# Gate and noise matrices laid out by the host function, the table's VectorE operations given out one at a time, four value loads in one slot

## The chip, the cores and the metric

The kernel runs on one NeuronCore of one Trainium2 chip. Its engines are called here PE (TensorE, with PEld for its weight loads), DVE (VectorE), ACT (ScalarE), POOL (GpSimd) and SP (SyncE, which only issues DMAs). The metric is the device time of one execution, in microseconds. A hardware profile of one execution gives start and duration of each instruction and what ended the wait before it.

## The reference

Two stages follow each other. First attention over 8 batches, 8 heads, 576 positions and head size 64: heads 0 to 3 see a window of the last 32 positions ("plain"), heads 4 to 7 every fourth of the last 128 ("dilated"). The result is then 4608 tokens of 512 values, which go to two of eight experts each:

```python
logits = x @ w_gate
noise_scale = np.log1p(np.exp(x @ w_noise))
noisy_logits = logits + noise_scale * noise
top2 = np.argpartition(-noisy_logits, 2, axis=1)[:, :2]
...
        h = np.maximum(x[mask] @ w1[e], 0.0)
        out[mask] += top2_w[mask, k, None] * (h @ w2[e])
```

`w_gate` and `w_noise` are 512x8, `noise` is 4608x8, `w1` 8x512x1024, `w2` 8x1024x512, all float32.

## The kernel before, in words

**Attention (0 to about 200 us).** Four units of two batches; each unit has two groups, the even one dilated (keys `kd`, values `vd`), the odd one plain (`kp`, `vp`); each group has three steps. So there are 24 steps, numbered from 0, and step 3 is the first of the first plain group. The main loop (L1015 to L1047) writes the engines' orders out by hand, several steps interleaved. In its turn a step does the following.

- `qk`: two matmuls write the mask into the score tile `s` (L361), then 48 small ones add keys times queries (L372). DVE takes the maximum `mx` (L377) and writes `a = s - mx` (L378); `a` has a single buffer.
- `expo`: ACT takes the exponential of `a` (L384). `ptr`: PE transposes it into `pp` (L398), ACT copies it to `pt` (L399).
- `pv`: values times `pt` into `o` (L416); then DVE's `den`, reciprocal and scaled `x` (L423, L425, L428). `x` has three buffers.
- two slots later `x` is copied in part by ACT (L436), stored to the DRAM scratch `xs` (L441, L443), transposed by PE (L451) and multiplied by the gate and noise matrix `wg` (L473).

Between these pieces stand calls of `micro` (nine a step) and two of `fillers`. `fillers(kb)` runs what `at(kb, f)` has put down for slot `kb` (two slots a step): loads for later groups, the setups and the starts of generators. `micro` gives the generators in the list `gens` turns, in their order in the list: after a `yield 0` a generator goes on, after `yield 1` it rests to the next slot, after `yield 3` the next generator has the turn. The generators build, for the tokens whose gate values are there, noisy logits, the two best experts and the positions in each expert's list, and POOL scatters these (L630) into the DRAM table `tab`, of 37376 rows of four words.

**SP's queue.** SP issues its DMAs in the order of the program. Each waits for the one eight places before it to land, besides its own conditions (buffers free, data ready), and those behind it wait with it. The order at the start: the loads of group 0, of group 0's values, then keys and queries of group 1, and then what the slots bring.

**The setups.** `setup_a` (slot 2) clears `wg` on POOL, loads gate and noise weights into it and the noise into `nz` by three POOL DMAs (L213 to L215), with the last dimension of 8 floats as the longest contiguous run in DRAM, and makes constants. `setup_b` (slot 4) computes, in 29 DVE operations on small integer tiles `tc` (L237 to L261), the row of `xs` that belongs to each token (`tokc`). `setup_c` (slot 5) makes the rows of padding, and `pads` (slots 6, 12 and 18) writes them in three pieces to `tab` by SP (L284), through one buffer, `free`.

**Pacing.** Before a group of scatters POOL copies one element of the newest `a` or `x` to `spacer` (L307), so that POOL doesn't run ahead of the steps. That copy is a reader of `a`, for which the next writing of `a` waits.

**Experts (about 200 us to the end).** The eight experts follow one another: tokens gathered by POOL from `xs` with lists out of `tab` (L773, L781), split in two parts of lower precision, multiplied up (L829), rectified, multiplied down (L871), scaled and scattered to the output.

Of the kernel before, what the change touches and what calls it, by code (L numbers as in the profile page):

```python
# [23 lines left out]
E = 8  # L24
# [4 lines left out]
NT = T // 128  # L29
# [14 lines left out]


@with_exitstack
def attention_moe_kernel(ctx, tc, qt, kp, kd, vpl, vdl, w_gate, w_noise, noise, w1, w2, out, CAPS=(1216, 1216, 1216, 1184, 1184, 1152, 1152, 1152), SPLITS=(0, 384, 896)):
    nc = tc.nc
    tensor, vector, scalar, gpsimd, sync = nc.tensor, nc.vector, nc.scalar, nc.gpsimd, nc.sync

# [149 lines left out]
    wg = acon.tile([128, 4, 32], F32, name="wg")  # L200
    nz = gat.tile([128, NT, E], F32, name="nz")
# [7 lines left out]
    warm(NWARM)  # L209

    def setup_a():
        gpsimd.memset(wg, 0.0)
        gpsimd.dma_start(wg[:, :, 0:E], w_gate.rearrange("(c p) e -> p c e", p=128))  # L213
        gpsimd.dma_start(wg[:, :, E:2 * E], w_noise.rearrange("(c p) e -> p c e", p=128))
        gpsimd.dma_start(nz, noise.rearrange("(t p) e -> p t e", p=128))  # L215
# [12 lines left out]

    def setup_b():


        gpsimd.memset(tokc, 0)
        gpsimd.iota(tokc[:, :, 3:4], pattern=[[128, NT], [0, 1]], base=0, channel_multiplier=1)
        t = tokc[:, :, 3]
        v, s, i0, z, a = (acon.tile([128, 2, NT], I32, name=f"tc{i}") for i in range(5))
        gpsimd.iota(v[:, 0].rearrange("p (s j) -> p s j", j=3), pattern=[[0, 12], [128, 3]], base=0, channel_multiplier=1)
        vector.tensor_scalar(a[:, 0], t, 2, None, op0=OP.bitwise_and)  # L237
        vector.tensor_scalar(v[:, 1], t, 2, None, op0=OP.logical_shift_right)
        vector.scalar_tensor_tensor(v[:, 1], a[:, 0], 72.0, v[:, 1], op0=OP.mult, op1=OP.add)
        for u in range(U):  # L240
            c = slice(NG * u, NG * u + NG)
            gpsimd.iota(s[:, 0, c].rearrange("p (s j) -> p s j", j=3), pattern=[[384, 3], [0, 3]],
                        base=384 * (6 * u + 3), channel_multiplier=0)
            vector.tensor_scalar(a[:, 0, c], t[:, c], float(TU * u + S), 144.0, op0=OP.is_ge, op1=OP.mult)
            vector.scalar_tensor_tensor(v[:, 1, c], v[:, 1, c], -288.0 * u, a[:, 0, c], op0=OP.add, op1=OP.add)
            vector.memset(s[:, 1, c], 2304 * u)
        for lim in (192.0, 384.0):
            vector.tensor_scalar(z[:, int(lim) // 384], v[:, 1], lim, None, op0=OP.is_ge)
        vector.tensor_tensor(z[:, 0], z[:, 0], z[:, 1], op=OP.add)
        vector.scalar_tensor_tensor(s[:, 1], z[:, 0], 384.0, s[:, 1], op0=OP.mult, op1=OP.add)  # L250
        vector.tensor_scalar(a[:, 0], t, 1, None, op0=OP.bitwise_and)
        vector.tensor_tensor(z[:, 0], a[:, 0], z[:, 0], op=OP.subtract)
        vector.scalar_tensor_tensor(v[:, 1], z[:, 0], 192.0, v[:, 1], op0=OP.mult, op1=OP.add)

        vector.tensor_tensor(i0, v, s, op=OP.add)
        vector.tensor_scalar(a, v, 31, None, op0=OP.bitwise_and)
        vector.tensor_tensor(i0, i0, a, op=OP.add)
        vector.tensor_scalar(a, v, 32, None, op0=OP.bitwise_and)
        vector.scalar_tensor_tensor(i0, a, -31.0 / 32, i0, op0=OP.mult, op1=OP.add)
        for c in range(2):  # L260
            vector.tensor_copy(tokc[:, :, c], i0[:, c])  # L261

    def setup_c():
# [7 lines left out]
        vector.tensor_scalar(pc[:, 1:2], pc[:, 0:1], 15, None, op0=OP.bitwise_and)  # L271
        vector.tensor_scalar(pc[:, 0:1], pc[:, 1:2], float(NR), None, op0=OP.mult)
        gpsimd.iota(pr[:, 0], pattern=[[1, NR]], base=0, channel_multiplier=0)
        vector.tensor_tensor(pr[:, 0], pr[:, 0], pc[:, 0:1].to_broadcast([128, NR]), op=OP.add)
        vector.tensor_scalar(pr[:, 1], pr[:, 0], 127, None, op0=OP.bitwise_and)
        vector.tensor_scalar(pr[:, 2], pr[:, 0], OROWS - T - 1, None, op0=OP.bitwise_and)
        tr = tab.rearrange("(p t) c -> p t c", p=128)

        def pads(a, b):
            padt = free[1][:, 0:TC * (b - a)].rearrange("p (a b) -> p a b", b=TC)  # L280
            gpsimd.memset(padt, 0)
            vector.tensor_copy(padt[:, :, 0:2], pr[:, 1, a:b].unsqueeze(2).to_broadcast([128, b - a, 2]))
            vector.tensor_scalar(padt[:, :, 3], pr[:, 2, a:b], float(T), None, op0=OP.add)
            sync.dma_start(tr[:, a:b], padt)  # L284

        for i in range(3):
            at(6 + 6 * i, lambda i=i: pads(NR * i // 3, NR * (i + 1) // 3))

    gens, early = [], [True]
    room, held, rate = [0], set(), [1]  # L290
# [51 lines left out]
    slot = [0]  # L342
# [571 lines left out]
    def at(kb, *fs):  # L914
        fill.setdefault(kb, []).extend(fs)
# [3 lines left out]
    for g in range(2 * U):  # L919
        s0 = 6 * g  # L920
        if g + 1 < 2 * U:
            for i, f in enumerate(v_loads(g + 1)):
                at(s0 + 3 + 2 * (i // 2), f)
        if g + 2 < 2 * U:
            for i, f in enumerate(qk_loads(g + 2, 2)):
                at(s0 + 7 + 2 * (i // 3), f)
# [72 lines left out]
    for kc in range(4):  # L999
        a, b = ((-3, 2), (-2, 3), (4, 6), (5, 7))[kc]  # L1000
# [242 lines left out]
```

## Time and profile before

| | us |
|---|---|
| three runs | 1074.11, 1074.55, 1068.03 |
| their median | 1074.11 |
| the profiled execution | 1067.71 |
| its span | 1066.0 |
| PE busy in the span | 1001.5 (94%) |
| DVE busy | 468.1 (44%) |
| ACT busy | 319.8 (30%) |
| POOL busy | 537.6 (50%) |

Times in rows of the profile count from the start of the span. A timeline row has start, duration, engine, line, operation, output and input tiles with shapes, the count of instructions in it, and in square brackets how long the engine stood idle before it and what released it. SPq rows are DMA issues on SP's queue. A row of stretches has start and end, the length, then busy time and count for PE, PEld, DVE, ACT and POOL, the clock granted to PE, the share of time that the DMA engines were busy and what they moved.

### The profile page before, as it was taken

To read this page: it belongs to the slowest core of one execution; us is meant where nothing else is said; L and a number is where in the kernel's file an instruction comes from. 1 tells how busy PE (TensorE), PEld (TensorE's weight loads), DVE (VectorE), ACT (ScalarE), POOL (GpSimd) and SP (SyncE) were. 2 spreads that over 40 slices of the span, in tenths; PEclk is the share of its full clock that TensorE was granted. 3 is DMA by queue.
4 is the path that set the end of the run, shared out by engine and by line. 5 is a ranking of instruction groups with operands and counts; after the bars stand their busy time and mean duration, and the time that the engine had idled before them with its cause. 6 is when DMAs were issued, how large, how long until landed. Compare 5 with 4: busy or idle time off the path is not lost. (4 is left out here: it accounts for less than half of the span.)

```text
span 1066.0 us, 18824 instructions
## 1 busy us (share of the span) xinstructions
PE 1001.5 (94%) x7275; PEld 844.3 (79%) x7276; DVE 468.1 (44%) x1088; ACT 319.8 (30%) x612; POOL 537.6 (50%) x737
## 2 busy tenths in 40 slices
PE   6897887879799999999999999999999999899996
PEld 4775665758588888979897988898888888798885
DVE  7784757633144534353425343534344433333221
ACT  7664646511022312241213121312232122222110
POOL 7004244576768467555545555466455644652112
PEclk9999998989899999999999999999999999999998
DMA  8999788652336336242724262426232623443123
GB/s 283 322 335 324 247 284 283 179 209 36 70 69 140 99 57 142 56 111 52 140 42 113 51 139 43 114 50 139 47 111 55 136 51 98 95 93 80 21 29 43
DMA packets 79214, 132.95 MB, mean 125 GB/s; under 512 B 31648, under 2 KB 41296, under 8 KB 77840
## 3 DMA queue, kind: packets, MB, share of 16 engines
q1 hardware_dynamic: 56768, 92.56, 27.9%
q0 software_dynamic: 22352, 39.15, 20.3%
q8 instruction: 58, 0.95, 0.4%
q14 instruction: 36, 0.29, 0.1%
HBM read 92.11 MB, written 39.54 MB: 124 GB/s over the span
## 5 line engine op out<-in xcount | busy, mean ns | idle before, releaser
L829 PE MATMUL up<-x,w1h 128*128 128x512 f32 (+4 forms) x1536 | 393.4, 342 | 4.8 <-DVE hl L835 2.6
L781 POOL DMA_INDIRECT g<-xs,ixi x258 | 268.9, 1042 | 84.3 <-issue 79.3
L829 PEld LDWEIGHTS up<-x,w1h 128*128 128x128 f32 x1536 | 270.4, 188 | 31.1 <-DVE hl L835 3.3
L829 PE MATMUL up<-x,w1l 128*128 128x384 f32 (+4 forms) x768 | 261.9, 341 | 0.0
L871 PE MATMUL dn<-w2h,hh 128*128 128x512 f32 x576 | 226.7, 394 | 1.6 <-issue 1.5
L871 PE MATMUL dn<-w2l,hh 128*128 128x512 f32 x576 | 226.6, 393 | 1.7 <-issue 0.9
L871 PE MATMUL dn<-w2h,hl 128*128 128x512 f32 x576 | 225.9, 392 | 1.7 <-issue 1.7
L835 DVE SCALAR_TENSOR_TENSOR hl<-up,hh 128x384 fp32r<-128x384 f32 (+2 forms) x192 | 106.6, 556 | 247.4 <-ACT hh L833 183.7
L833 ACT ACTIVATE hh<-up 128x384 fp32r<-128x384 f32 (+4 forms) x192 | 94.6, 498 | 298.6 <-PE up L829 235.5
L848 POOL DMA_INDIRECT out_rows<-y,ixs x67 | 107.4, 1602 | 142.5 <-DVE y L880 123.9
L829 PEld LDWEIGHTS up<-x,w1l 128*128 128x128 f32 x768 | 144.1, 188 | 11.8
L880 DVE TENSOR_SCALAR y<-dn,ixs 128x512 f32<-128x512 f32 x63 | 47.3, 751 | 188.7 <-PE dn L871 158.3
L871 PEld LDWEIGHTS dn<-w2l,hh 128*128 128x128 f32 x576 | 109.1, 189 | 26.2 <-issue 3.5
L871 PEld LDWEIGHTS dn<-w2h,hl 128*128 128x128 f32 x576 | 109.1, 189 | 24.7 <-issue 2.2
L871 PEld LDWEIGHTS dn<-w2h,hh 128*128 128x128 f32 x576 | 109.3, 190 | 23.5 <-issue 1.4
L800 ACT CAST x<-xr 128x512 fp32r<-128x512 f32 x67 | 40.5, 604 | 216.6 <-DVE xr L798 173.3
L307 POOL COPY spacer<-hh 1x1 f32<-1x1 f32 x73 | 25.9, 355 | 130.9 <-ACT hh L833 130.6
L630 POOL DMA_INDIRECT tab<-en,si x72 | 72.9, 1013 | 31.2 <-issue 26.1
L801 DVE TENSOR_TENSOR x<-xr,x 128x512 fp32r<-128x512 f32 x67 | 44.7, 667 | 17.9 <-ACT x L800 13.0
L710 DVE TENSOR_TENSOR w1l<-ws,w1h 128x1024 fp32r<-128x1024 f32 x32 | 38.8, 1217 | 21.1 <-issue 11.3
L708 ACT CAST w1h<-ws 128x1024 fp32r<-128x1024 f32 x32 | 33.1, 1049 | 45.1 <-DMA ws<-in_moe_w 45.0
L798 DVE STREAM_TRANSPOSE xr<-g 128x512 f32<-128x512 f32 x67 | 45.7, 682 | 1.7 <-DMA g<-xs,ixi 1.7
(187 smaller groups left out, 846.3 us busy)
## 6 DMA issues: line engine op xcount, KB each, us to landing
ws<-in_moe_w SPq DMA_DIRECT2D x36, 512.0 KB
ws<-in_moe_w SPq DMA_DIRECT2D x112, 128.0 KB
out_rows<-zero SPq DMA_DIRECT2D x38, 256.0 KB
vd<-in_vdl SPq DMA_DIRECT2D x24, 390.0 KB
vp<-in_vpl SPq DMA_DIRECT2D x16, 585.0 KB
qt<-in_qt SPq DMA_DIRECT2D x14, 576.0 KB
xs<-x SPq DMA_DIRECT2D x24, 256.0 KB
kt<-in_kd SPq DMA_DIRECT2D x16, 320.0 KB
```

Of the source, the lines that this page charges most:

```text
L630: ins = gpsimd.indirect_dma_start(out=tab, out_offset=bass.IndirectOffsetOnAxis(ap=si[:, kq, t:t + 1], axis=0), in_=en[:, kq, t], in_offse ...
L710: return lambda: vector.tensor_tensor(b, s, a.bitcast(F32), op=OP.subtract)
L781: gpsimd.indirect_dma_start(out=g[:, j], out_offset=None, in_=xq, in_offset=bass.IndirectOffsetOnAxis(ap=IX[e][1][:, r0 // 32 + j:r0 // 32 ...
L798: vector.transpose(xr[:, :, 0:rn].rearrange("p c (g t) -> p g c t", t=32), g[:, 0:n].rearrange("p g (c d) -> p g c d", d=32))
L800: scalar.copy(xh[:, :, o:o + rn], xr[:, :, 0:rn])
L801: return lambda: vector.tensor_tensor(xl[:, :, o:o + rn], xr[:, :, 0:rn], xh[:, :, o:o + rn].bitcast(F32), op=OP.subtract)
L829: tensor.matmul(p[:, 0:n], lhsT=a[:, 128 * f:128 * f + 128], rhs=b[:, kc, 0:n], start=(i == 0), stop=(i == 11))
L833: scalar.activation(hh[:, f, 0:n], p[:, 0:n], AF.Relu)
L835: vector.scalar_tensor_tensor(hl[:, f, 0:m], p[:, 0:m], 0.0, hh[:, f, 0:m].bitcast(F32), op0=OP.max, op1=OP.subtract)
L848: ins = gpsimd.indirect_dma_start(out=out, out_offset=bass.IndirectOffsetOnAxis(ap=sc[0:rn, t, 1:2], axis=0), in_=y[0:rn], in_offset=None, ...
L871: tensor.matmul(p[0:rn], lhsT=a[:, f, o:o + rn], rhs=b[:, f % 2], start=(i == 0), stop=(i == 23))
L880: vector.tensor_scalar(y[0:rn], p[0:rn], wsc, None, op0=OP.mult)
```

## The change

1. `wg`, 128x4x32 floats with the two matrices and zeros, and `nz`, 128x36x8, are put into their on-chip order by `kernel()` on the host, and each is loaded by one contiguous DMA on SP. `wg` goes out behind the values of group 0 and ahead of the keys of group 1, the noise at slot 6. POOL's memset of `wg` and its three DMAs are gone.
2. `setup_b`, `setup_c` and `pads` become one generator, started at slot 4, with a `yield 3` behind each DVE operation. POOL's operations in them stand where they stood. The DMA of a padding piece is put down two slots after its operations. While this generator lives, those behind it in the list get their turns after it.
3. The four value loads of group 1 all go out at slot 3, where it was two at slot 3 and two at slot 5. Later groups are as they were.

```diff
 def setup_a():
-        gpsimd.memset(wg, 0.0)
-        gpsimd.dma_start(wg[:, :, 0:E], w_gate.rearrange("(c p) e -> p c e", p=128))
-        gpsimd.dma_start(wg[:, :, E:2 * E], w_noise.rearrange("(c p) e -> p c e", p=128))
-        gpsimd.dma_start(nz, noise.rearrange("(t p) e -> p t e", p=128))
         gpsimd.memset(ones, 1.0)
...
         vector.tensor_scalar(a[:, 0], t, 2, None, op0=OP.bitwise_and)
+        yield 3
         vector.tensor_scalar(v[:, 1], t, 2, None, op0=OP.logical_shift_right)
+        yield 3
...
             gpsimd.memset(padt, 0)
             vector.tensor_copy(padt[:, :, 0:2], pr[:, 1, a:b].unsqueeze(2).to_broadcast([128, b - a, 2]))
+            yield 3
             vector.tensor_scalar(padt[:, :, 3], pr[:, 2, a:b], float(T), None, op0=OP.add)
-            sync.dma_start(tr[:, a:b], padt)
+            yield 3
+            at(slot[0] + 2, lambda: sync.dma_start(tr[:, a:b], padt))
 
         for i in range(3):
-            at(6 + 6 * i, lambda i=i: pads(NR * i // 3, NR * (i + 1) // 3))
+            yield from pads(NR * i // 3, NR * (i + 1) // 3)
+            for _ in range(4):
+                yield 1
...
-                at(s0 + 3 + 2 * (i // 2), f)
+                at(s0 + 3 + (2 * (i // 2) if g else 0), f)
...
-    at(4, setup_b)
-    at(5, setup_c)
+    def setup():
+        yield from setup_b()
+        yield from setup_c()
+
+    at(4, lambda: gens.append(setup()))
+    at(6, lambda: sync.dma_start(nz, noise))
     for f in v_loads(0):
         f()
+    sync.dma_start(wg, wgn)
     for f in qk_loads(1):
         f()
...
+    wgn = np.zeros((4, 128, 32), np.float32)
+    for i, name in enumerate(("moe_w_gate", "moe_w_noise")):
+        wgn[:, :, E * i:E * i + E] = np.reshape(inputs[name], (4, 128, E))
+    given["wgn"] = wgn.transpose(1, 0, 2)
+    given["noise"] = np.reshape(inputs["moe_noise"], (NT, 128, E)).transpose(1, 0, 2)
```

SP's queue at the start, from the last value loads of group 0 to the first loads of group 2. Before:

```order
L120 DMA vd<-in_vdl 64x1560 x6
L108 DMA kt_97<-in_kp 64x2432 x2
L111 DMA qt_99<-in_qt 128x2304
L125 DMA vp_94<-in_vpl 64x2340 x2
L441 DMA xs<-x 256x1x256
L443 DMA xs<-x 64x1x256 x2
L125 DMA vp_95<-in_vpl 64x2340 x2
L284 DMA tab<-free 128x388
L441 DMA xs<-x 256x1x256
L443 DMA xs<-x 64x1x256 x2
L108 DMA kt_98<-in_kd 64x1280 x2
```

And now (L464 and L466 are the stores that were L441 and L443, L1005 and L1002 the two new loads):

```order
L120 DMA vd<-in_vdl 64x1560 x6
L1005 DMA wg<-in_wgn 128x128
L108 DMA kt_97<-in_kp 64x2432 x2
L111 DMA qt_99<-in_qt 128x2304
L125 DMA vp_94<-in_vpl 64x2340 x2
L125 DMA vp_95<-in_vpl 64x2340 x2
L464 DMA xs<-x 256x1x256
L466 DMA xs<-x 64x1x256 x2
L1002 DMA nz<-in_noise 128x288
L464 DMA xs<-x 256x1x256
L466 DMA xs<-x 64x1x256 x2
L108 DMA kt_98<-in_kd 64x1280 x2
```

The matrix `wg` stands ahead of the keys and queries of group 1, the second pair of `vp` loads ahead of the first stores, the noise between the first two steps' stores, and the first padding piece has left this part of the queue.

DVE where the table's operations were one block, now, in step 3 (`tc` are the table's tiles; L446, L448 and L451 are `den`, the reciprocal and `x`, formerly L423, L425 and L428):

```order
L233 TENSOR_SCALAR tc_395<-tokc 128x36
L446 TENSOR_SCALAR den<-o 128x6 x2
L235 TENSOR_SCALAR tc_391<-tokc 128x36
L448 RECIPROCAL den<-den 128x12
L237 SCALAR_TENSOR_TENSOR tc_391<-tc_395,tc_391 128x36
L451 TENSOR_TENSOR x<-o,den 128x384 x2
```

Before, all 29 of them stood ahead of this `den`; now one stands ahead of it, one ahead of the reciprocal, one ahead of `x`, and the others follow in this manner.

POOL at the first scatters into the table, with the semaphores that each row waits for. Before (L307 and L309 are the spacer, L630 the scatter):

```order
L307 COPY spacer<-a 1x1 [waits DVE_49]
L630 DMA tab<-en_1337,si_1406 37376x4 [waits DMAHW0_49,DVE_49]
L307 COPY spacer<-x 1x1 [waits DVE_49,Pool_49]
L630 DMA tab<-en_1337,si_1406 37376x4
L309 MEMSET spacer 1x1 [waits Pool_49]
L630 DMA tab<-en_1337,si_1406 37376x4
L307 COPY spacer<-a 1x1 [waits DVE_49,Pool_49]
```

And now (L330, L332 and L653 are the same three lines):

```order
L330 COPY spacer<-a 1x1 [waits DVE_49]
L653 DMA tab<-en_1361,si_1432 37376x4 [waits DVE_49]
L330 COPY spacer<-x 1x1 [waits DVE_49,Pool_49]
L653 DMA tab<-en_1361,si_1432 37376x4 [waits DMAHW0_49]
L332 MEMSET spacer 1x1 [waits Pool_49]
L653 DMA tab<-en_1361,si_1432 37376x4
L330 COPY spacer<-a 1x1 [waits DVE_49,Pool_49]
```

The wait for a DMA of SP's (`DMAHW0`, the third padding piece) has moved from the first scatter to the second. SP's issue of that piece, which had the waits `DMAHW0, DVE, Pool`, now has `DMAHW0, DMASW0, Pool`: the `DMASW0` is the first scatter, which has to land before the piece goes out.

More of the change, by code (lines that the diff above doesn't have):

```diff
@@ L46, in attention_moe_kernel @@
 @with_exitstack
-def attention_moe_kernel(ctx, tc, qt, kp, kd, vpl, vdl, w_gate, w_noise, noise, w1, w2, out, CAPS=(1216, 1216, 1216, 1184, 1184, 1152, 1152, 1152), SPLITS=(0, 384, 896)):
+def attention_moe_kernel(ctx, tc, qt, kp, kd, vpl, vdl, wgn, noise, w1, w2, out, CAPS=(1216, 1216, 1216, 1184, 1184, 1152, 1152, 1152), SPLITS=(0, 384, 896)):
     nc = tc.nc
@@ L244, in setup_b @@
             vector.tensor_scalar(a[:, 0, c], t[:, c], float(TU * u + S), 144.0, op0=OP.is_ge, op1=OP.mult)
+            yield 3
             vector.scalar_tensor_tensor(v[:, 1, c], v[:, 1, c], -288.0 * u, a[:, 0, c], op0=OP.add, op1=OP.add)
+            yield 3
             vector.memset(s[:, 1, c], 2304 * u)
+            yield 3
         for lim in (192.0, 384.0):
             vector.tensor_scalar(z[:, int(lim) // 384], v[:, 1], lim, None, op0=OP.is_ge)
+            yield 3
         vector.tensor_tensor(z[:, 0], z[:, 0], z[:, 1], op=OP.add)
+        yield 3
         vector.scalar_tensor_tensor(s[:, 1], z[:, 0], 384.0, s[:, 1], op0=OP.mult, op1=OP.add)
+        yield 3
         vector.tensor_scalar(a[:, 0], t, 1, None, op0=OP.bitwise_and)
+        yield 3
         vector.tensor_tensor(z[:, 0], a[:, 0], z[:, 0], op=OP.subtract)
+        yield 3
         vector.scalar_tensor_tensor(v[:, 1], z[:, 0], 192.0, v[:, 1], op0=OP.mult, op1=OP.add)
+        yield 3
         vector.tensor_tensor(i0, v, s, op=OP.add)
+        yield 3
         vector.tensor_scalar(a, v, 31, None, op0=OP.bitwise_and)
+        yield 3
         vector.tensor_tensor(i0, i0, a, op=OP.add)
+        yield 3
         vector.tensor_scalar(a, v, 32, None, op0=OP.bitwise_and)
+        yield 3
         vector.scalar_tensor_tensor(i0, a, -31.0 / 32, i0, op0=OP.mult, op1=OP.add)
+        yield 3
         for c in range(2):
             vector.tensor_copy(tokc[:, :, c], i0[:, c])
+            yield 3
     def setup_c():
@@ L271, in setup_c @@
         vector.tensor_scalar(pc[:, 1:2], pc[:, 0:1], 15, None, op0=OP.bitwise_and)
+        yield 3
         vector.tensor_scalar(pc[:, 0:1], pc[:, 1:2], float(NR), None, op0=OP.mult)
+        yield 3
         gpsimd.iota(pr[:, 0], pattern=[[1, NR]], base=0, channel_multiplier=0)
         vector.tensor_tensor(pr[:, 0], pr[:, 0], pc[:, 0:1].to_broadcast([128, NR]), op=OP.add)
+        yield 3
         vector.tensor_scalar(pr[:, 1], pr[:, 0], 127, None, op0=OP.bitwise_and)
+        yield 3
         vector.tensor_scalar(pr[:, 2], pr[:, 0], OROWS - T - 1, None, op0=OP.bitwise_and)
+        yield 3
         tr = tab.rearrange("(p t) c -> p t c", p=128)
@@ L282, in pads @@
             vector.tensor_copy(padt[:, :, 0:2], pr[:, 1, a:b].unsqueeze(2).to_broadcast([128, b - a, 2]))
+            yield 3
             vector.tensor_scalar(padt[:, :, 3], pr[:, 2, a:b], float(T), None, op0=OP.add)
-            sync.dma_start(tr[:, a:b], padt)
+            yield 3
+            at(slot[0] + 2, lambda: sync.dma_start(tr[:, a:b], padt))
         for i in range(3):
-            at(6 + 6 * i, lambda i=i: pads(NR * i // 3, NR * (i + 1) // 3))
+            yield from pads(NR * i // 3, NR * (i + 1) // 3)
+            for _ in range(4):
+                yield 1
     gens, early = [], [True]
@@ L1186, in attention_moe_kernel @@
                 pend.pop()()
-_NAMES = ['moe_w_gate', 'moe_w_noise', 'moe_noise', 'moe_w1', 'moe_w2']
+_NAMES = ['moe_w1', 'moe_w2']
 def _layouts(q, k, v):
```

## The prediction

> **What bounds the kernel now.** I read the head of the page, then busy time by stage, then the TensorE (PE) timeline in the stage that the change touches, and last what PE waited for there. The head's span:
>
> ```profile
> span 1066.0 us, 18824 instructions
> ```
>
> The profiled execution took 1067.71 us, 1.7 us more than its span. Busy times in five stretches (start:end and length, then busy us of PE, PEld, DVE, ACT, POOL, then PE clock, DMA share, GB/s):
>
> ```profile
> 15.40:29.60 14.20, 10.15 (x231) 8.17 (x231) 10.07 (x42) 6.75 (x16) 8.14 (x24) 1.00 1.02 340
> 29.60:76.00 46.40, 45.58 (x1016) 37.36 (x1018) 35.24 (x128) 33.34 (x86) 0.92 (x3) 1.00 0.94 330
> 76.00:200.00 124.00, 98.53 (x1815) 74.41 (x1807) 73.82 (x279) 69.14 (x170) 51.78 (x90) 0.93 0.84 277
> 200.00:330.00 130.00, 115.67 (x547) 95.30 (x548) 51.92 (x165) 27.27 (x50) 89.37 (x143) 0.93 0.45 112
> 330.00:1066.00 736.00, 723.17 (x3608) 625.15 (x3606) 284.88 (x450) 171.35 (x287) 375.95 (x460) 0.99 0.39 82
> ```
>
> PE is the bound, and in 29.6 to 76 and from 330 on it hardly pauses: 0.8 us idle of 46.4, and 12.8 of 736. So what the change touches before 29.6 us can at most move everything behind it earlier by a constant. It adds nothing to the expert stage, whose instructions stand in the same order. The stretch 15.4 to 29.6 has 4.05 us of idle PE, and the timeline says where:
>
> ```profile
> 24.96 0.29 PE L416 MATMUL o<-vd,pt 128*32 128x130 f32 x2
> ...
> 25.51 0.50 PE L361 MATMUL s<-mask,identb 128*128 128x512 bf16 x2
> 29.61 1.52 PE L372 MATMUL s<-kt,qt 128*32 128x128 f32 x48 [3.60 <-DMA qt<-in_qt]
> 31.05 0.88 PE L398 MATMUL pp<-ident,pe 128*128 128x128 f32 x6
> 31.77 0.82 PE L451 MATMUL xtp<-ident,x 128*128 128x128 f32 x6
> ...
> 34.99 1.52 PE L372 MATMUL s<-kt,qt 128*32 128x128 f32 x48
> ...
> 40.38 0.86 PE L372 MATMUL s<-kt,qt 128*32 128x128 f32 x24
> ```
>
> One wait of 3.60 us: step 3, the first of the plain group, has its mask matmuls done at 26.0 and waits for that group's queries. From there steps repeat every 5.39 us (34.99 to 40.38) with no PE wait. This wait is the only thing in reach; the most that its removal gives is 3.60 us, 0.3% of the time.
>
> **Part 1, the small loads (expected gain).** What DMA moved in those microseconds, and what was issued (SP's and POOL's issue rows):
>
> ```profile
> 16.00:20.00 4.00, 3.54 (x91) 2.79 (x80) 1.92 (x2) 1.81 (x3) 3.68 (x5) 1.00 1.04 430
> 20.00:24.00 4.00, 4.00 (x82) 3.24 (x82) 3.27 (x7) 2.05 (x6) 3.68 (x20) 1.00 1.03 365
> 24.00:28.00 4.00, 2.01 (x56) 1.53 (x48) 3.42 (x27) 2.34 (x7) 0.18 (x1) 1.00 1.02 203
> 28.00:32.00 4.00, 2.40 (x57) 2.23 (x58) 3.66 (x15) 1.00 (x3) 0.00 (x0) 1.00 0.99 380
> ```
> ```profile
> 15.27 0.33 SPq L111 DMA_DIRECT2D qt<-in_qt  x1
> ```
> ```profile
> 16.72 1.00 POOL L213 DMA_DIRECT2D wg<-in_moe_w_gate  x1 [0.32 <-POOL wg L212]
> 17.72 0.82 POOL L214 DMA_DIRECT2D wg<-in_moe_w_noise  x1
> 18.51 1.86 POOL L215 DMA_DIRECT2D nz<-in_moe_noise  x1
> ```
>
> The DMA engines are full throughout (share 0.99 to 1.04), but what they move falls from 430 GB/s to 203 after POOL has issued its three loads, which by their shapes are 512 + 512 + 4608 runs of 32 bytes (16, 16 and 144 KB). The queries were issued at 15.27, ahead of all three, and were still incomplete at 29.6. I price the small loads by the bytes that were not moved at the rate of the first row: (430 − 365) × 4 + (430 − 203) × 4 + (430 − 380) × 1.6 us = 0.26 + 0.91 + 0.08 = 1.25 MB, at 430 GB/s 2.9 us. Not all of this need be their work (the xs stores have 256-byte and longer runs and stay), so it is an estimate. The new contiguous load of the gate matrix, 64 KB with its zeros, stands in SP's queue ahead of the group's keys and costs 0.15 us at that rate. Net 2.75 us; the queries then land near 26.8, and PE waits 0.85 us instead of 3.60. The noise load, 144 KB contiguous, goes out at slot 6 after the queries, where nobody waits for it for tens of microseconds: nothing.
>
> [...]
>
> With PE released, is something else late? VectorE's (DVE's) rows, and ScalarE's (ACT's) copy of what they make:
>
> ```profile
> 24.04 0.19 DVE L237 TENSOR_SCALAR tc<-tokc 128x36 int32<-128x36 int32 x1
> ...
> 28.48 0.29 DVE L261 COPY tokc<-tc 128x36 int32<-128x36 int32 x2
> 28.66 0.23 DVE L423 TENSOR_SCALAR den<-o 128x6 f32<-128x6 f32 x2
> ...
> 34.34 0.23 DVE L423 TENSOR_SCALAR den<-o 128x6 f32<-128x6 f32 x2 [0.45 <-PE o L416]
> 34.61 0.23 DVE L425 RECIPROCAL den<-den 128x12 f32<-128x12 f32 x1
> 34.87 1.02 DVE L428 TENSOR_TENSOR x<-o,den 128x384 f32<-128x384 f32 x2
> 36.60 0.96 DVE L377 TENSOR_REDUCE mx<-s 128x12 f32<-128x768 f32 x1 [0.71 <-PE s L372]
> 37.67 0.96 DVE L378 TENSOR_TENSOR a<-s,mx 128x768 f32<-128x768 f32 x1
> ```
>
> ```profile
> 30.23 0.83 ACT L436 COPY x<-x 32x256 f32<-32x256 f32 x2 [3.62 <-DVE x L428]
> ```
>
> The 29 operations of the token table stand as one block from 24.04 to 28.77 (4.73 us, 0.163 each), and `den` of step 1 stands behind them although its last `o` matmuls ended at 25.25 (24.96 + 0.29). Were the block still there, x of step 1 would be late for its transposes, and releasing the queries would give little. The change breaks the block up, so `den`, reciprocal and x take their 1.5 us from 25.2, with two or three table operations between (0.4 us) to 27.2, and ScalarE's copy after it (0.83 us) ends near 28.0; PE wants it for its transposes 2.2 us after the query matmuls begin (29.61 to 31.77), so at 28.2 if these began at 26.0, and at 29.0 if at 26.8. So both edits are needed for the gain, and both are made. I take 2.75 us; bounds 0.8 (x or `a` late by 2 us after all) and 3.6.
>
> **Part 2, the operations spread (small cost).** The generator gives one operation at each turn; the loop has nine turns a step, so 9 × 0.163 = 1.5 us a step over steps 3 to 6. In a steady step DVE works 3.58 us of 5.39 (the five rows from 34.34 to 38.63, without the 0.71 before `mx`) and is idle 1.81 us. It fits, barely. An operation standing between `mx` and `a` delays the subtraction by 0.16; I charge 0.25 us in all (PE catches up as it is never held by more than one such operation). If the cover were gone (each operation on PE's path), 34 operations × 0.163 = 5.5 us; the least is 0, since the block's own 4.73 us goes.
>
> **Part 3, four value loads at slot 3, and POOL free earlier.** The second pair stood in SP's queue behind the first xs stores and now stands ahead of them. It is 1.17 MB, 2.7 us at 430 GB/s, so the stores land up to 2.7 us later; the buffer of x that they read is one of three and is rewritten two steps on, over 10 us. The pairs stand behind the queries in the queue, as now. Nothing, with 0.5 us either way. POOL loses 3.7 us of issue at 16.7 to 20.4, and nobody waited for it: nothing.
>
> **Part 4, the third stretch of padding (a new wait).** The pad rows of the table were written before the first scatter into it. Now the third piece comes after it in program order: SP's `tab<-free` waits for scatter 1, and scatter 2 on POOL waits for that piece. Behind scatter 2 on POOL stand scatter 3 and the spacer copy that reads `a`; the next subtraction into `a`, a single buffer, waits for that copy; and SP's next xs stores stand behind the waiting `tab<-free`. Rows:
>
> ```profile
> 50.03 0.35 SPq L284 DMA_DIRECT2D tab<-free  x1
> 55.39 0.42 POOL L281 MEMSET free<- 128x392 int32 x1 [17.21 <-DMA tab<-free]
> ...
> 77.92 1.11 POOL L630 DMA_INDIRECT tab<-en,si  x1 [1.81 <-DVE si L627]
> 79.38 1.01 POOL L630 DMA_INDIRECT tab<-en,si  x1 [0.17 <-issue]
> 80.69 0.97 POOL L630 DMA_INDIRECT tab<-en,si  x1 [0.22 <-issue]
> 81.68 1.11 SPq L120 DMA_DIRECT2D vd<-in_vdl  x2
> 88.62 0.96 DVE L378 TENSOR_TENSOR a<-s,mx 128x768 f32<-128x768 f32 x1
> 93.68 0.50 PE L361 MATMUL s<-mask,identb 128*128 128x512 bf16 x2
> 154.48 0.57 SPq L441 DMA_DIRECT2D xs<-x  x1
> 168.32 1.01 POOL L773 DMA_INDIRECT g<-xs,ixf  x1 [8.40 <-DMA xs<-x]
> ```
>
> SP issues the piece behind the vd pair, near 82.8 (81.68 + 1.11). Such a piece was seen landed 5.36 us after its issue (50.03 to 55.39), so scatter 2 starts at 88.2 instead of 79.38. Scatters 2 and 3 take 2.28 us (79.38 to 80.69 + 0.97); with the copy behind them that is 90.8, and the subtraction starts there instead of at 88.62 and ends at 91.8. PE's next writing of `s`, which this frees, is at 93.68: 1.9 us to spare. Cost 0. The other bound is the slowest landing in reach, 13.84 us (an xs store issued at 154.48, the gather that waits for it at 168.32): then the slip past the spare is 13.84 − 5.36 − 1.9 = 6.6 us.
>
> **The sum.** −2.75 + 0.25 + 0 + 0 = −2.5 us: the profiled execution would go from 1067.7 to 1065.2. The three runs shown (1068.03, 1074.11, 1074.55) and this execution lie in two groups six apart, and I can't tell in which one the new kernel is timed; I subtract from the mean of the four, 1071.1, and forecast 1068.5, half a per cent under the median of 1074.11 shown. Whatever is under 1% (10.7 us) counts as no change.
>
> **The rivals.**
> 1. The padding chain decides. For: it is a new dependence through two queues at a time when DMA is 0.84 busy; SP holds the vd and xs issues behind it too. Against: the only such landing shown took 5.36 us. A landing over 7.3 us after issue costs, one over 9.8 us eats the gain, and the slowest gives −2.5 + 6.6 = +4.1: 1075, slower than before. 0.15.
> 2. The spread operations cancel the gain: DVE has 0.3 us of slack a step left, and with 0.6 us lost in each of four steps 2.4 us are gone: 1071. For: the arithmetic of part 2 is tight. Against: PE has `s` to reduce 0.71 us before DVE is asked for it. 0.17.
> 3. A larger gain. The stretch 76 to 200 has 25.5 us of idle PE, and DMA there is busy at 0.84; if the earlier start and the missing block shift loads so that a fifth of it goes, 1068.5 − 5 = 1063.5. For: nothing but the size of that idle time. 0.13.
> 4. The change does nothing for the queries: the deficit of 1.25 MB isn't the small loads' doing (the xs stores, or reads and writes mixed), and the queries land at 29.6 as before, less DVE's block: 1071. The two pieces that speak for it: the noise and gate bytes are still loaded, and DMA share stays 1.0. 0.10. [...]
>
> **How the numbers follow.** Forecast 0.45, the rivals 0.15, 0.17, 0.13, 0.10. Their centres span 1063.5 to 1075; the two groups add 3 on either side, and rival 3 a little more (it has no row that bounds it but the idle time): 1058 to 1078 holds 8 in 10. Faster by over 1% (under 1063.4) takes most of rival 3 and a few of the forecast's in the low group: 0.13. Slower by over 1% (over 1084.8) only an unforeseen stall reaches: 0.04. Within: 0.83.
>
> **What would show it.** Right: step 3's kt,qt matmuls start by 27.5 with under 1.5 us of wait for queries; DMA in 24 to 28 is above 330 GB/s; no run of table operations on DVE longer than two; the step time from step 4 on stays 5.4; the second scatter starts some 10 us behind the first, and PE's mask matmul after it doesn't wait for DVE. Wrong: steps 4 to 7 at 5.7 us or more (rival 2); PE waiting near 94 for `s` from a late `a` (rival 1); the queries still landing near 29 (rival 4); a change of PE's idle time in 76 to 200 by more than 3 us, which would carry the result away from this sum in either direction.

## The result: slower by 0.6%

Nine runs of each kernel give a median of 1078.45 us for the changed kernel (1071.45 to 1082.81) and 1072.22 for the kernel before (1068.03 to 1076.83): ratio 1.0058, interval 1.0034 to 1.0082. The forecast was 1068.5, 0.5% under the median that was then known; the time lies just outside the range, on the other side. The profiled execution took 1078.45 us, 10.7 more than that of before.

The changed kernel's stretches (columns as before: length, busy PE, PEld, DVE, ACT, POOL, PE clock, DMA share, GB/s), then DMA in the four microseconds in question:

```profile
15.40:29.60 14.20, 12.96 (x290) 10.61 (x290) 8.45 (x23) 8.04 (x20) 4.27 (x20) 1.00 1.02 422
29.60:76.00 46.40, 38.90 (x809) 30.96 (x809) 29.33 (x112) 26.51 (x69) 0.42 (x1) 0.96 0.86 295
76.00:200.00 124.00, 97.06 (x1861) 74.39 (x1852) 74.63 (x305) 67.66 (x170) 44.03 (x79) 0.93 0.82 260
...
24.00:28.00 4.00, 3.22 (x95) 2.62 (x90) 1.90 (x11) 2.88 (x9) 0.00 (x0) 1.00 1.02 420
```

Up to 29.6 us it is as forecast: PE busy 12.96 us instead of 10.15, and DMA at 420 GB/s where it moved 203. Then 29.6 to 76, where PE had been idle for 0.8 us, has 7.5 us of idle PE. PE's rows say where the first of it is:

```profile
26.52 0.75 PE L395 MATMUL s<-kt,qt 128*32 128x128 f32 x19 [0.78 <-DMA qt<-in_qt]
...
43.09 0.41 PE L395 MATMUL s<-kt,qt 128*32 128x128 f32 x3 [3.44 <-issue]
43.43 0.87 PE L421 MATMUL pp<-ident,pe 128*128 128x128 f32 x6
44.14 1.17 PE L474 MATMUL xtp<-ident,x 128*128 128x128 f32 x6
45.23 2.80 PE L439 MATMUL o<-vp,pt 128*32 128x130 f32 x44
```

The wait for queries is 0.78 us (forecast 0.85, before 3.60). In step 5 PE then stops for 3.44 us with 45 of its 48 score matmuls done, and nothing that the profile names is missing ("issue", the profile's word for time in which an engine waited for nothing that it shows). After it the same matmuls take longer: 44 of `o` 2.80 us, where the kernel before has

```profile
23.46 1.57 PE L416 MATMUL o<-vd,pt 128*32 128x130 f32 x44
```

The windows around it, then DMA by queue between 39.6 and 43.1:

```profile
40.00:44.00 4.00, 0.91 (x8) 0.71 (x8) 0.47 (x1) 0.00 (x0) 0.00 (x0) 1.00 1.01 401
44.00:48.00 4.00, 4.00 (x61) 3.42 (x63) 2.66 (x7) 2.56 (x5) 0.00 (x0) 0.57 0.98 379
```
```profile
DMA packets 461, 1.36 MB, mean 390 GB/s; under 512 B 69, under 2 KB 219, under 8 KB 460
q8 instruction: 1, 0.02, 1.6%
```

A block of instructions (0.02 MB, the queue named instruction) is loaded inside PE's pause, while the data loads keep the DMA engines full (a share of 1.01 from 40 to 44); from 33 to 40.4 no such load stands in the trace. No row names it as what PE waits for; that it is rests on the profiles of the experiments below. They and this one have 14 such stops of over 1 us in steps 4 to 7, and in 13 of them a load on that queue began 2.2 to 2.5 us before PE went on (in the other one, in e8, 3.1 us); here it began at 40.6, and PE went on at 43.09. On these counts I call the 14 stops for instructions. What is late is the load: it began 6.8 us after PE had passed the same place of step 4 (33.86). In the 14 stops that distance is about 4.2 to 6.8 us, in the four profiles of the kernel before about 0.1 to 3.7 us.

The granted clock then falls to 0.57 for four microseconds (44 to 48). So this pause costs more than its length: step 5 took 10.81 us instead of 5.38. Not every stop has such a fall behind it, and its length alone doesn't tell which: seven of the 14 stops were followed by a granted clock of 0.64 or less, the shortest of them 2.14 us long (e9 below), and seven were not, the longest of them 3.17 us (e5); nor was the wait of 3.60 us in the kernel before (1.00 from 28 to 52).

Two more places, both of the padding. The rows of DVE, POOL and SP:

```profile
63.71 0.26 DVE L301 COPY free<-free 128x194 int32<-128x194 int32 x1 [4.82 <-POOL free L300]
...
83.43 1.11 SPq L120 DMA_DIRECT2D vd<-in_vdl  x2
91.77 0.35 SPq L305 DMA_DIRECT2D tab<-free  x1
...
85.35 1.21 POOL L653 DMA_INDIRECT tab<-en,si  x1 [2.28 <-DVE si L650]
93.94 0.98 POOL L653 DMA_INDIRECT tab<-en,si  x1 [7.19 <-DMA tab<-free]
...
96.39 0.96 DVE L401 TENSOR_TENSOR a<-s,mx 128x768 f32<-128x768 f32 x1 [3.72 <-POOL spacer L330]
```

DVE stands 4.82 us before its padding copy, because POOL's memset of the one buffer (begun at 63.3) waits for the first piece (issued at 56.35) to land; behind the copy stand `den` and `x` of step 7. And SP is held from 84.5 (83.43 + 1.11) to 91.77 for the first scatter to land (issued 85.35), the second scatter waits for the third piece, and the subtraction into `a` waits 3.72 us for the spacer copy. PE's mask matmuls of step 13 begin as that subtraction ends (96.39 + 0.96), 0.99 us late, and more pauses follow:

```profile
97.40 0.48 PE L384 MATMUL s<-mask,identb 128*128 128x512 bf16 x2 [0.99 <-issue]
97.81 0.41 PE L395 MATMUL s<-kt,qt 128*32 128x128 f32 x2
98.57 0.27 PE L395 MATMUL s<-kt,qt 128*32 128x128 f32 x1 [0.35 <-issue]
99.38 0.37 PE L395 MATMUL s<-kt,qt 128*32 128x128 f32 x1 [0.54 <-issue]
```

Step 13 takes 16.35 us (7.77 in the kernel before). Seven pauses of this kind between its matmuls add up to 4.6 us, and from 100 to 106 the granted clock is 0.51. The first four aren't stops like that of step 5, since from 92 to 105 no block of 0.02 MB is loaded on the instruction queue. Eight scatters leave POOL meanwhile (93.94 to 105.98). What PE waits for there is not known.

While SP is held the DMA engines have less to do:

```profile
80.00:100.00 20.00, 16.56 (x338) 12.74 (x336) 12.21 (x46) 11.04 (x27) 6.86 (x12) 0.98 0.72 228
```

In the kernel before the same stretch has a share of 0.98 and 306 GB/s.

### The profile page after: what moved, and what is told of

Read it like the earlier page. It is cut to its first block, busy times and chain, and to the rows that moved or that the text cites. A ratio compares the mean times of both kernels' runs of the same rounds, so it can differ in the third digit from the quotient of the medians.

```text
span 1076.8 us, 18825 instructions
## 1 busy us (share of the span) xinstructions
PE 1004.3 (93%) x7275; PEld 848.5 (79%) x7276; DVE 467.3 (43%) x1088; ACT 319.8 (30%) x612; POOL 534.4 (50%) x733
## 3 DMA queue, kind: packets, MB, share of 16 engines
q1 hardware_dynamic: 57056, 92.77, 27.9%
## 5 line engine op out<-in xcount | busy, mean ns | idle before, releaser
L852 PEld LDWEIGHTS up<-x,w1h 128*128 128x128 f32 x1536 | 273.4, 189 | 32.2 <-issue 4.0
L653 POOL DMA_INDIRECT tab<-en,si x72 | 73.5, 1020 | 36.2 <-issue 18.3
L330 POOL COPY spacer<-hh 1x1 f32<-1x1 f32 x73 | 26.8, 368 | 128.1 <-ACT hh L856 127.8
L395 PE MATMUL s<-kt,qt 128*32 128x128 f32 x1152 | 40.9, 280 | 7.4 <-issue 6.2
```

What stands on the lines that cost most here:

```text
L395: tensor.matmul(s[32 * qd:32 * qd + 32, e], lhsT=QV[ty][:, b, x, 32 * ub:32 * ub + 32], rhs=KV[ty][:, :, b, x, 32 * ub:32 * ub + 64], star ...
L653: ins = gpsimd.indirect_dma_start(out=tab, out_offset=bass.IndirectOffsetOnAxis(ap=si[:, kq, t:t + 1], axis=0), in_=en[:, kq, t], in_offse ...
L852: tensor.matmul(p[:, 0:n], lhsT=a[:, 128 * f:128 * f + 128], rhs=b[:, kc, 0:n], start=(i == 0), stop=(i == 11))
```

## The experiments

The runs went to several chips. On some the kernel before takes 1072 to 1074 us, on others 1039, where many of the steps from 11 to 20 take 6 us that take about 8 on the former; why is not known. Ratios are against the kernel before on the same chip, and steps are compared between chips of one kind only. Length of steps, from one start of the mask matmuls to the next (one profile each, us; the profiled executions of a0, e3, e6 and e8 are the slowest of theirs):

| kernel | chip | step 3 | steps 4 to 7 | step 8 | steps 11 to 13 | ratio, interval |
|---|---|---|---|---|---|---|
| before | 1072 | 9.05 | 23.06 | 6.00 | 24.96 | |
| b0, before | 1074 | 9.14 | 22.77 | 6.01 | 26.20 | |
| b2, before | 1072 | 8.71 | 22.77 | 6.00 | 27.88 | |
| b1, before | 1039 | 8.34 | 23.13 | 6.01 | 18.02 | |
| changed | 1072 | 6.51 | 29.12 | 9.34 | 30.53 | 1.0058, 1.0034 to 1.0082 |
| a0, changed | 1074 | 6.81 | 26.41 | 7.15 | 30.38 | 1.0014, 1.0002 to 1.0025 |
| e3 | 1039 | 8.46 | 26.02 | 7.32 | 21.42 | 1.0059, 1.0036 to 1.0081 |
| e4 | 1039 | 6.64 | 27.70 | 6.01 | 20.16 | 1.0067, 1.0044 to 1.0091 |
| e5 | 1074 | 6.41 | 27.53 | 6.00 | 30.57 | 1.0046, 1.0030 to 1.0062 |
| e6 | 1074 | 5.43 | 27.06 | 12.51 | 34.85 | 1.0115, 1.0092 to 1.0138 |
| e8 | 1039 | 10.71 | 29.00 | 6.01 | 18.59 | 1.0034, 1.0013 to 1.0055 |
| e1 | 1039 | 6.80 | 23.64 | 6.12 | 22.25 | 1.0025, 0.9998 to 1.0053 |
| e15, same as e1 | 1039 | 6.36 | 28.22 | 6.00 | 17.76 | 1.0008, 0.9983 to 1.0032 |
| e12 | 1072 | 5.83 | 23.40 | 6.00 | 22.03 | 0.9982, 0.9956 to 1.0007 |
| e14, same as e12 | 1039 | 6.27 | 29.38 | 6.00 | 17.75 | 1.0011, 0.9983 to 1.0038 |
| e2 | 1039 | 8.33 | 23.14 | 6.01 | 17.52 | 1.0019, 0.9999 to 1.0038 |
| e9 | 1039 | 7.20 | 30.60 | 6.01 | 18.30 | 1.0032, 1.0010 to 1.0054 |
| e11 | 1072 | 5.55 | 25.58 | 9.19 | 23.74 | 0.9999, 0.9984 to 1.0013 |
| e13 | 1072 | 10.59 | 23.31 | 6.00 | 26.00 | 1.0016, 0.9999 to 1.0032 |

**The padding as before (e1).** The pieces at slots 6, 12 and 18 again, with their operations in one go, and `setup_c` first in the generator:

```diff
-            yield from pads(NR * i // 3, NR * (i + 1) // 3)
-            for _ in range(4):
-                yield 1
+            at(6 + 6 * i, lambda i=i: pads(NR * i // 3, NR * (i + 1) // 3))
...
-        yield from setup_b()
-        yield from setup_c()
+        yield from setup_c()
+        yield from setup_b()
```

> The changed kernel with one part undone: the three padding pieces are again made in one go at slots 6, 12 and 18 with their DMA issued at once, and setup_c's five operations stand ahead of setup_b's in the generator so that the pieces have what they need. Layouts, value loads and the spreading of setup_b stay. Theory A (the padding chain is the loss: DVE's padding copy waits 4.8 us for POOL's memset and so for a landing near 63, and the second scatter waits 7.2 us for the third piece): step 8 back from 9.3 to about 6.0 us, step 13 back from 16.4 towards 8, time 1068 to 1071, ratio to before 0.996 to 0.999. Rival B (PE's wait for instructions, 3.4 us at 43.09, is what the removed wait for queries turned into, and the padding waits are covered elsewhere): step 5 stays at 10 to 11 us, time 1074 to 1079, ratio above 1.002.

Measured 1.0025: above A's range, just over B's limit, but without B's stop in step 5 (5.38 us). Both padding waits are gone (step 8 6.12 us, step 13 6.01), and the loss is half or less of e3's and e4's on the same chip, but a gain isn't there.

**The layouts alone (e2), the generator alone (e3), the value loads as before (e4).** e2 is the kernel before with the two contiguous loads, e3 the kernel before with the generator, e4 the changed kernel with

```diff
-                at(s0 + 3 + (2 * (i // 2) if g else 0), f)
+                at(s0 + 3 + 2 * (i // 2), f)
```

> The kernel before with the two contiguous loads alone (gate and noise matrices laid out, one DMA each on SP); the table's operations, the padding and the value loads as before. Theory A: the queries land about 2.7 us earlier (wait near 0.8 us instead of 3.6), but DVE's block of 29 operations still makes x of step 1 late, so that step 3 shortens by 0.5 to 1.5 us only, and the time is 1070 to 1073, ratio 0.997 to 1.001. Rival B: PE's wait for instructions takes the place of the wait for queries in one of steps 3 to 6, ratio 1.000 to 1.002 whatever step 3 gains.

> The kernel before with the generator alone (table operations and padding given out one at a time, padding DMA two slots later); small loads by POOL and value loads as before. Theory A: the loss without the gain: the two padding waits are there (4 to 5 us on DVE, 5 to 8 us on POOL's second scatter), ratio 1.006 to 1.012, 1079 to 1085. Rival B: with the wait for queries back, PE doesn't outrun its instructions, no wait for them in steps 4 to 6, and the time is that of before, ratio 0.998 to 1.003.

> The changed kernel with the value loads of group 1 again two at slot 3 and two at slot 5. Theory A: the same as the changed kernel, 1.004 to 1.008, with both padding waits. Rival C (the four value loads at once hold up PE's instruction loads): no wait for instructions in step 5, which falls from 10.8 to about 6, and the ratio falls to 1.000 to 1.003.

e2: the queries' wait is 1.73 us, but step 3 takes 8.33 us, no less than b1's 8.34 on a chip of the same kind, since DVE's block is still there; A had it shorter by 0.5 to 1.5. The time, 1.0019, is just outside A's range and in B's, without B's stop in its profile. Its DMA at 24 to 28 us is near that of the changed kernel, and e3, with the small loads, has 197, so the small loads were what had held it at 203:

```profile
24.00:28.00 4.00, 2.27 (x67) 1.82 (x60) 3.45 (x26) 2.38 (x8) 0.00 (x0) 1.00 1.00 399
```

e3 has the whole loss without the layouts (1.0059, just under A's range). B falls, in its ratio and by a stop of 2.16 us in step 6, which came although the wait for queries was back (3.00 us). e4 is as slow as the changed kernel (1.0067), with the chain of the third piece and without DVE's wait in step 8. Its step 5 is back at 5.93 us, as C had it, but the stop has moved to step 6 (2.42 us), so C falls.

**Which link of the padding (e5, e6, beside b0 and a0).** e5 gives the second piece its own part of the buffer, so that DVE waits for no landing. e6 lets POOL instead of SP issue the third piece.

```diff
-            padt = free[1][:, 0:TC * (b - a)].rearrange("p (a b) -> p a b", b=TC)
+            o = 400 if a == NR // 3 else 0
+            padt = free[1][:, o:o + TC * (b - a)].rearrange("p (a b) -> p a b", b=TC)
...
-            at(slot[0] + 2, lambda: sync.dma_start(tr[:, a:b], padt))
+            at(slot[0] + 2, lambda: (sync, gpsimd)[b == NR].dma_start(tr[:, a:b], padt))
```

> The kernel before, unchanged, for its profile beside the profiles of the experiments. All theories: the 3.6 us wait for queries in step 3, no wait of DVE for the padding, SP's three padding issues near 34, 50 and 70, and DMA moving over 300 GB/s from 80 to 100.

> The changed kernel, unchanged, beside the experiments. All theories: ratio 1.004 to 1.008; SP issues the third padding piece near 88 to 92, some 8 us behind the vd load before it; DMA falls to 210 to 230 GB/s between 80 and 100.

> The changed kernel with one line other: the second padding piece has its own region of the buffer, so that POOL's memset for it waits for no landing and DVE's padding copy waits for nothing. The third piece still stands behind the first scatter. Theory A1 (DVE's wait of 1.2 to 4.8 us in steps 8 to 10 is the larger part of the loss): ratio falls to 1.002 to 1.004. Theory A2 (the third piece is the loss: SP is held some 8 us by it while DMA is what bounds this stage): ratio stays at 1.005 to 1.008, DMA at 80 to 100 still 210 to 230 GB/s.

> The changed kernel with the third padding piece issued by POOL instead of SP, at the same place of the program: POOL waits for the first scatter to land, issues the piece, and the second scatter waits for it as before; SP waits for nothing there. Theory A2 (SP held): DMA at 80 to 100 rises to 300 GB/s and more, and the ratio falls to 1.001 to 1.004. Rival (POOL's own wait, with the spacer copy and the late subtraction into the scores' single buffer behind it): the subtraction near 91 to 96 still waits 2.5 to 4 us for the spacer copy, and the ratio stays at 1.005 to 1.008.

On this chip the changed kernel itself lost only 0.14%, less than expected; its executions lie between 1070.6 and 1082.6, those of before between 1071.2 and 1075.2. e5 has step 8 back at 6.00 us and is no faster (1.0046, between the ranges of A1 and A2): DVE's wait is real in the profile, but taking it away gained nothing here, so A1 falls. e6 has SP free and DMA at 302 GB/s from 80 to 100, as A2 wanted, and is the slowest of all. Its rows:

```profile
85.82 1.21 POOL L653 DMA_INDIRECT tab<-en,si  x1 [2.28 <-DVE si L650]
94.12 0.62 POOL L305 DMA_DIRECT2D tab<-free  x1 [7.10 <-DMA tab<-en,si]
94.74 0.18 POOL L330 COPY spacer<-x 1x1 f32<-1x1 f32 x1
99.80 1.02 POOL L653 DMA_INDIRECT tab<-en,si  x1 [4.88 <-DMA tab<-free]
...
102.29 0.96 DVE L401 TENSOR_TENSOR a<-s,mx 128x768 f32<-128x768 f32 x1 [9.16 <-POOL spacer L330]
```

The chain is longer by some 5 us (14 us between the two scatters, where it was 8.6), the subtraction waits 9.16 us instead of 3.72, and the ratio rises to 1.0115. PE itself then waits 7.08 us for `a` ahead of step 13. So letting SP go doesn't help when POOL, and with it `a`, stands longer. How much of the 1.0115 is the chain's, e6 doesn't say: its step 8 takes 12.51 us, where DVE's copy for the second piece waits 5.87 us.

**The chain given to the kernel before (e8, beside b1), and taken from the changed kernel (e9).** e8 is the kernel before with the DMA of the third piece alone put down later (at slot 21 instead of 18, three slots and not two); e9 is e5 with the third piece right behind the second.

```diff
-            sync.dma_start(tr[:, a:b], padt)
+            go = lambda: sync.dma_start(tr[:, a:b], padt)
+            at(slot[0] + 2, go) if b == NR else go()
```
```diff
-            for _ in range(4):
+            for _ in range(4 * (i == 0)):
                 yield 1
```

> The kernel before, unchanged, for its profile beside the three that follow. All theories: as before, step 13 at 6 to 8 us, DMA from 80 to 100 above 300 GB/s.

> The kernel before with one thing other: the third padding piece's DMA is put down two slots later, so that it stands behind the first scatter and the second scatter behind it, as in the changed kernel; its operations stay at slot 18. Theory A2 (this chain through SP and POOL is the changed kernel's loss): ratio 1.003 to 1.007, DMA from 80 to 100 down to 210 to 260 GB/s, the second scatter some 8 us behind the first. Rival (the loss is in the spreading and in DVE's waits): ratio 0.999 to 1.002.

> The changed kernel with two regions for the first two padding pieces (so DVE waits for no landing) and the third piece made right behind the second, ahead of the first scatter; layouts, spreading and value loads as changed. Theory A2: the chain is gone, ratio 0.997 to 1.001, that is 3 to 5 us under the changed kernel, with step 13 as in the kernel before. Rival (the spreading itself costs, by later turns for the gate's operations): ratio stays at 1.003 to 1.006.

e8 is slower by 0.34% (0.13 to 0.55), inside A2's range: as a difference of whole times, the chain by itself costs 1.4 to 5.7 us. Its rows have it as in the changed kernel, the second scatter at 92.97 behind the first at 85.45, and the subtraction waiting 1.81 us. The profiled execution doesn't show the price where I expected it: steps 11 to 13 are only 0.6 us longer than b1's. 8.2 of its 8.9 us above b1's stand in steps 3 to 7, where the two programs are still the same; most of that is a stop for instructions in step 6, at the end of the scores again, with a granted clock of 0.50 behind it (52 to 56):

```profile
47.32 1.51 PE L373 MATMUL s<-kt,qt 128*32 128x128 f32 x46
51.82 0.59 PE L373 MATMUL s<-kt,qt 128*32 128x128 f32 x2 [2.98 <-issue]
52.33 1.54 PE L399 MATMUL pp<-ident,pe 128*128 128x128 f32 x6
```

e9 is at 1.0032, not at the 1.000 that A2 wanted: without the chain and without DVE's wait, 0.3% remains. Its profile has two stops for instructions, 2.89 and 2.14 us, in steps 5 and 6. So the chain is, by these times, one loss and not the only one.

**Loads of group 2 later (e11), SP let go earlier (e13), neither padding nor value loads (e12), beside b2.** e11 is e9 with the keys and queries of group 2 a step later. e13 is the kernel before with the DMA of the first piece four slots later, so that SP, which stood 9 us ahead of it, goes on. e12 is e1 with the value loads as before, so that layouts and spreading remain.

```diff
-                at(s0 + 7 + 2 * (i // 3), f)
+                at(s0 + (7 if g else 9) + 2 * (i // 3), f)
```
```diff
-            sync.dma_start(tr[:, a:b], padt)
+            go = lambda: sync.dma_start(tr[:, a:b], padt)
+            at(slot[0] + 3, go) if a == 0 else go()
```

> The kernel before, unchanged, for its profile beside the three that follow. All theories: the wait for queries in step 3, no wait of PE for instructions over 1 us in steps 4 to 7 (none in the three profiles of it so far).

> The kernel of e9 (no padding wait on DVE, third piece ahead of the scatters) with the keys and queries of group 2 loaded one step later (slots 9 and 11 instead of 7 and 9). Theory E (with the first padding piece gone from its old place SP hands out group 2's loads 3 to 5 us earlier, and PE's instruction load for step 5 or 6 stands behind them): no wait for instructions over 1 us in steps 4 to 7, and a ratio of 0.996 to 1.000. Rival F (the wait comes by chance or from elsewhere in the stream): a wait of 2 to 5 us in steps 4 to 7 as in the seven profiles with the generator, ratio 1.002 to 1.006.

> The kernel before with the DMA of the first padding piece four slots later; its operations stay at slot 6. SP is no longer held for it until 34 us. Theory E: group 2's loads go out 2 to 4 us earlier, a wait for instructions of 2 to 5 us appears in steps 4 to 7, ratio 1.002 to 1.006. Rival F: nothing changes, ratio 0.999 to 1.001.

> The changed kernel with the padding as before (its pieces at slots 6, 12 and 18, setup_c ahead of setup_b) and the value loads as before, so that only the layouts and the spreading of setup_b remain. Theory E: SP is held for the first piece as in the kernel before, no wait for instructions in steps 4 to 7, step 3 shorter by 2 to 2.5 us, ratio 0.997 to 1.000. Rival G (the gain of step 3 is given back in any case, since the later loads and the first gather set the pace): ratio 1.000 to 1.003.

e11 comes back to the kernel before (0.9999), where E had it, but a stop of 2.41 us stands in its step 6, where E had none, and DVE waits for a memset in step 8 again (3.45 us, the step 9.19; the third piece shares the first one's region). e13 has no stop and is at 1.0016, between the two theories, though its loads of group 2 begin at 33.3 us, 3.3 earlier than b2's. So the earlier loads don't bring the stop about by themselves: E isn't shown. e12 had no wait of PE over 0.15 us in steps 3 to 6 (step 3 5.83 us) and the lowest ratio of all, 0.9982, within its uncertainty the same as before.

**The same two again on one chip (e14, e15).**

> The kernel of e12 again (layouts and spreading of setup_b alone; padding and value loads as before), beside the kernel of e1 on one chip. Theory H (the gain of step 3 remains where nothing else is changed): ratio 0.995 to 1.000, no wait for instructions over 1 us in steps 4 to 7. Rival G (it is given back in any case): 1.000 to 1.003.

> The kernel of e1 again: as the one above, with the four value loads of group 1 at slot 3. Theory I (the value loads at once cost): ratio 0.002 to 0.005 above the one above. Rival: the same as the one above within 0.0015; then the difference of e1 and e12 was that of two chips.

1.0011 and 1.0008: the value loads make no difference, and H is not borne out, in its ratio or its stops. Both profiles have the stop now that e1's and e12's had not or hardly:

```profile
27.41 1.83 PE L391 MATMUL s<-kt,qt 128*32 128x128 f32 x48 [0.50 <-DMA qt<-in_qt]
...
41.82 0.41 PE L391 MATMUL s<-kt,qt 128*32 128x128 f32 x3 [1.25 <-issue]
...
50.02 0.54 PE L391 MATMUL s<-kt,qt 128*32 128x128 f32 x3 [2.41 <-issue]
```

(e14; the stop is again at three matmuls from the end.) So for one and the same kernel the stop comes in some executions and not in others. The four comparisons of these two kernels average 1.0007, with a half-width of 0.0013 (root of the sum of the four squared half-widths, by four): the 0.9977 that the 2.5 us of a shorter step 3 alone would give lies outside.

**Fewer loads (e10).** The kernel before without the value loads of the third dilated group (group 4). It leaves these loads out and so computes something else; only its steps are compared.

```diff
-        if g + 1 < 2 * U:
+        if g + 1 < 2 * U and g + 1 != 4:
             for i, f in enumerate(v_loads(g + 1)):
```

> The kernel before without the value loads of the third dilated group (six loads of 390 KB, 2.3 MB, issued between 80 and 92; that group is computed with the values of the one before, so its tokens are routed otherwise). Theory D (from 60 to 110 the loads are what bounds the steps): steps 11 to 14 shorten by 4 to 6 us together, and PE's pauses there go. Rival: PE's pauses there are its own (instructions), steps 11 to 14 change by under 1.5 us. The total also has what the other routing does to the experts, so only the steps up to 170 us are compared.

Steps 11 to 14 take 23.76 us, b1's 24.72: theory D falls on this chip. The loads are not what sets the pace there, although b1's DMA share from 80 to 100 is 0.97. On the slower chips (1072 to 1074 us), where these steps are longer, it was not tried.

## Why the prediction failed

**Part 1, the small loads: right.** The forecast of 2.75 us for the queries and 0.85 us of remaining wait came out as 2.82 (3.60 to 0.78), and DMA at 24 to 28 us rose from 203 to 420 GB/s. That the two agree to 0.1 us is partly luck: the wait is 2.06, 2.43 and 3.25 us in the other three profiles of the kernel before. Both edits are needed: e2 and e3, with one of them each, have step 3 at 8.33 and 8.46 us (b1 8.34); e1, e14 and e15, with both, at 6.27 to 6.80, and e12 at 5.83 (b2 8.71).

**Part 2 and part 3, the spread operations and the value loads: right.** Step 4 took 5.39 us in e1 and e12 with `setup_b` spread, as in the kernel before; 0.25 us was charged in all. (The sign named for rival 2, steps 4 to 7 at 5.7 us or more, could not tell: in the kernel before they average 5.77, since its steps 6 and 7 take 6.29 and 6.00.) The value loads at once make no difference (e4, and e15 beside e14).

**"What the change touches before 29.6 us can at most move everything behind it earlier by a constant": wrong.** I took the 0.8 us of idle PE in 29.6 to 76 as a sign that the stage has PE work alone to do. It had no named wait, but the profiles show blocks of 0.02 MB on the instruction queue, and in 13 of the 14 stops PE went on 2.2 to 2.5 us after one had begun. Where such stops came, they took 2.3 to 5.0 us of steps 4 to 7 in all, and seven of the 14 had a granted clock of 0.64 or less behind them; steps 4 to 7 then take 25.6 to 30.6 us, and 22.8 to 23.1 in the kernel before. In steps 4 to 7 a stop of over 1 us stands in 9 of the 11 profiles of kernels whose loads were laid out and whose DVE block was spread (not in e1 and e12), and in 2 of the 9 others (e3 and e8; in none of the four of the kernel before). That the absent wait is what brings the stop on is only argued from these counts, and some of the record is against it: e3 and e8 had the wait (3.00 and 3.67 us) and the stop, e8 in a part of the program that is still the kernel before's. From one such place to the next PE has one step to go in either kernel, so PE being earlier doesn't by itself leave the load less time. What delays the load in one execution and not in another stays open.

**Part 4, the third piece: "Cost 0", and that failed.** The chain itself was not underrated. The forecast had the second scatter 10.3 us behind the first (77.92 to 88.2); measured are 8.6 (85.35 to 93.94). Two errors inside it work against each other: "SP issues the piece behind the vd pair, near 82.8" gave no time to the first scatter's landing, which was named as a wait (SP issued at 91.77, 6.4 us after the scatter began), and the piece's own landing was put at 5.36 us and took 2.2 at most (91.77 to 93.94). What failed is the spare of 1.9 us that the cost was set against. It was read off the kernel before, where step 13's mask matmuls begin 17.2 us behind step 11's (76.49 to 93.68). In the changed kernel steps 11 and 12 are shorter and step 13's come 14.2 us behind (83.22 to 97.40). The subtraction, 13.2 us behind step 11's start where the forecast had 14.3, was now in the way: it waited 3.72 us, and PE 0.99 us for it (2.63 in a0, 1.89 in e5). That is rival 1 in its sign and its chain, but not by the slow landing of the piece that it counted on. More than half of what step 13 has over the kernel before (4.6 of 8.6 us) is the pauses between single matmuls, which nothing in the prediction had and whose cause is open. a0 and e5 have them too, with step 13 at 15.20 and 16.21 us; e3, e4 and e8, with the same chain on the faster chips, don't, and their step 13 takes 7.03, 7.04 and 6.07. e8 prices the chain at 3.5 us (1.4 to 5.7) as a difference of whole times.

**A wait not seen.** DVE's padding copy now stands in DVE's order behind POOL's memset, which waits for the piece before it to land: 4.82 us in step 8. In the kernel before the same wait stood on POOL alone, with DVE's copy in a slot far behind it. I had followed the piece to its queue and not to the buffer it comes from. e5, without this wait, was no faster.

**The sum.** A gain of 2.5 us that most profiles give back by stops for instructions, and 3 to 4 us for the chain. The six comparisons with the third piece behind the first scatter on SP (changed, a0, e3, e4, e5, e8) average a ratio of 1.0046, the eight without it (e1, e2, e9, e11 to e15) 1.0012. On the slower chips steps 11 to 13 show it: 30.4 to 30.6 us in the changed kernel, a0 and e5, 25.0 to 27.9 in the kernel before. On the faster ones they do so less clearly: 21.4 and 20.2 in e3 and e4, 18.6 in e8 and 18.0 in b1, but 22.3 in e1, which has no chain. The spread between chips (1.0014 to 1.0058 for the same changed kernel) is as large as the effects and isn't explained. No variant was shown to be faster than the kernel before.

## What to carry to other kernels

When a step's order is changed, follow each buffer and each ordered write to the landing that releases it, and give that landing a time from a row: a wait that is named and not timed is priced at zero. A spare that is read off the old timeline holds only if the steps ahead of it keep their lengths. A wait that is removed early in a busy stream need not be worth its length (here 2.82 us of it went, and stops of 2.3 to 5.0 us stood behind it in most profiles); look for pauses put down to "issue" close behind, at the same instruction, and for loads on the instruction queue beside them. And measure the parts apart on one chip, since here the whole differed more from chip to chip than most of its parts did from zero.

## What the runs showed of the hardware

PE's stops for instructions had not been in my reckoning for this stage: there are 14 of over 1 us in steps 4 to 7 of the 20 profiles, 1.25 to 3.44 us each, all of them 45 or 46 matmuls into a step's 48. In 13 of them PE went on 2.2 to 2.5 us after a load of 0.02 MB had begun on the instruction queue. In the changed kernel the data loads beside it moved 390 GB/s (39.6 to 43.1). The two stops priced here cost their length and then some: 3.44 us made step 5 of the changed kernel 5.43 us longer, with the clock at 0.57 for four microseconds, and 3.17 us in e5, with the clock at 1.00 behind it, made it 3.57 us longer. An indirect scatter of one row per partition took 6.4 us from its issue to the landing that SP waited for (85.35 to 91.77), in the changed kernel.
